# Row maxima of two key chunks taken as a couple: relu of their difference on ScalarE, one fused add-and-max on VectorE

## The chip, the cores and the metric

The kernel runs on one core of one Trainium2 chip. The metric is the device time of one execution in microseconds (us). A core has five engines that each run their own instruction queue in order and wait for each other through semaphores: TensorE (PE, with PEld for its weight loads), VectorE (DVE), ScalarE (ACT), GpSimd (POOL) and SyncE (SP), which here only issues DMAs. Matmuls write to PSUM, eight banks of 128 partitions x 512 float32 values; VectorE and ScalarE read them from there.

## The reference

```python
def _A_ref(x, wqkv, wo):                      # S = 2048, D = 512, H = 32 heads of Dh = 16
    qkv = (x @ wqkv).reshape(B, S, 3, H, Dh).transpose(2, 0, 3, 1, 4)
    q, k, v = qkv[0], qkv[1], qkv[2]
    scores = einsum("bhqd,bhkd->bhqk", q, k) * Dh ** -0.5
    p = softmax(scores, axis=-1)
    o = einsum("bhqk,bhkd->bhqd", p, v)
    return o.transpose(0, 2, 1, 3).reshape(B, S, D) @ wo

def _B_ref(x, w1, b1, w2, b2):                # F = 1792
    h = layernorm(x)
    u = gelu(einsum("bsd,sf->bdf", h, w1) + b1)
    return (einsum("bdf,fs->bds", u, w2) + b2).transpose(0, 2, 1)

xn = layernorm(x)
return x + _A_ref(xn, ...) * silu(_B_ref(xn, ...))
```

Attention over 32 heads, a token-mixing MLP, and a gated sum. Inputs and outputs are float32.

## The kernel before

**Precision.** A float32 operand is kept as two float32r parts, an upper one and the remainder (`sub`, L75). A product of two such operands takes three matmuls, or one with a contraction three times as long: `load_qk` (L97) lays the 16 rows of a head's q and k in 48 rows as (upper, upper, lower) against (upper, lower, upper).

**Preparation.** The first part (to L355) normalises x in four chunks of 512 tokens, turns it, and makes q, k and v. For each chunk there are four q parts and four k parts, of 128 rows each; a part's twelve matmuls go to a PSUM bank, ScalarE copies the upper half into a tile `sg`, VectorE subtracts the lower one, and a DMA writes both to HBM (`q_d`, `k_d`). Between the parts VectorE works off a list `todo`: the normalisation of the next chunk (`first`) and a second one for the mixer (`second`), whose result ScalarE and GpSimd split into the tiles `hb`. `hb` takes all sixteen slots of the pool `hu` at the start.

**The steps.** The rest works on pairs of heads, one on the array's rows 0 to 63 and one on 64 to 127, so that a matmul of either head runs beside one of the other. The loop over `s` (L944 on) makes one step out of two counts. Softmax is done over transposed scores (keys on the partitions), so its row maxima have to be known first, and they run `LEAD` = 20 counts ahead of the scores. One step has four maxima and four scores for each of the two heads, and work for both:

- the maxima (`max_of`, L378): queries of one block of 128 against the chunks 0 to 3 of 512 keys, each a matmul (L387) into a bank `mx` and a `tensor_reduce` (L391) on VectorE into a column of `mxp`
- the scores (`score`): a matmul (L757) into a bank `sc`, and an Exp on ScalarE (L762). Two extra rows of q hold the negated maximum
- two value bursts, each for both heads (`values`, eight matmuls at L773), from scores of the step before
- and some products of the mixer (L911), each split into two matmuls of 64 rows, one on each head's rows

The banks `mx` and `sc` are three each, handed round in order: a matmul into a bank waits for the reader of the product three before it in the same pool. The accumulators `av` and `dn` have one bank each.

`wanted` says how many mixer products a step gets: mostly six, otherwise five, four or two. All of them go in one run (a burst of mixer products) on one head's rows first, the lead's, and then in another on the other's. The order in a step is written out by hand in `ORDERS`; D is a mixer product, m a maxima product, s a score product. The first string is that of the lead, the second that of the other head, and the pairs are issued one by one; the number is the pair ahead of which the value burst of the middle stands:

```python
2: ("smsmDDsmsm", "msmsmsmsDD", 3),
4: ("sDDDDmsmsmsm", "msmsmsmDDDDs", 6),
6: ("DDDDDDsmsmsmsm", "msmsmsmsDDDDDD", 7),
```

So a step falls into two halves, each ahead of one value burst, and `lead` is turned round in each step that has mixer products. Of a step with six products, the first half holds the other head's four maxima and three of its scores, and one score of the lead; the second half the lead's four maxima.

After eight steps `max_rows` (L393) takes the maximum over the four columns of `mxp`, and `turn` moves it into the rows of q (a transpose at L402, a copy, two GpSimd instructions and four DMAs on GpSimd's queue).

**Before and after the steps.** Ten steps come first with maxima and mixer products alone (`first_maxima`), and ten follow the last maxima, with scores and the output product (`rest`, matmuls at L886). The last pair of heads is finished by `own` (L606): its `move_in` brings the first half of that pair's result into an operand tile with four DMAs on GpSimd's queue, and sets `own_done`, for which the generator `rest` waits ahead of the products that read the tile.

`later` and `after(n, f)` put off `f` to the n-th call of `run_later`; there are two calls in each step.

Of the kernel before, what the change touches and what calls it, by code (L numbers as in the profile page):

```python
# [21 lines left out]
def tile_attention_token_mixer(ctx, tc, x, wqkv, wo, w1, b1, w2, b2, out):  # L22
    nc = tc.nc
# [31 lines left out]
    q_d = [dram.tile([P, 2, S], F32R, name=f"q_d{g}") for g in range(ND)]  # L55
    k_d = [dram.tile([P, 2, S], F32R, name=f"k_d{g}") for g in range(ND)]
    v_d = dram.tile([NB, P, NP * 48], F32, name="v_d")
    u_d = [dram.tile([P, 2, D], F32R, name=f"u_d{i}") for i in range(NF)]
# [13 lines left out]
    xv = x.rearrange("(b p) d -> p b d", p=P)  # L72
    hb = [hu.tile([P, 2, D], F32R, name="hu") for _ in range(NB)]

# [12 lines left out]

    qs, ks, vps = {}, {}, {}

# [7 lines left out]
    def load_qk(p):  # L97
        if p > 1:
            qs[p], ks[p] = qs[p - 2], ks[p - 2]
        q, k = qs[p], ks[p]  # L100
        for a in range(2):
            g, r0 = divmod((2 * p + a) * DH, P)
            rows = slice(r0, r0 + DH)
            o = 64 * a

            for n in range(2):
                move(k[o + DH * n : o + DH * (n + 1), :], k_d[g][rows, n, :])
                move(q[o + DH * n : o + DH * (n + 1), :], q_d[g][rows, 0, :])
            move(k[o + 2 * DH : o + 3 * DH, :], k_d[g][rows, 0, :])
            move(q[o + 2 * DH : o + 3 * DH, :], q_d[g][rows, 1, :])  # L110
# [40 lines left out]
    with (  # L151
# [88 lines left out]
        def second(c):  # L240
            def then(b, o):
                h = hb[4 * c + b]
# [28 lines left out]
        for c in range(NC):  # L271
# [23 lines left out]
            for n, (part, g) in enumerate(order):  # L295
                m = slice(g * P, (g + 1) * P)
                ps = bank()
                for w, z in ((wh, 0), (wh, 1), (wl, 0)):
                    for kd in range(ND):
# [60 lines left out]
    sm = pool("sm", 2, reuse_waits="tile")  # L360
    el = pool("el", 2, reuse_waits="tile")

    later = []
# [13 lines left out]

    def max_of(u, half, a, pl=ps_mx, nm="mx"):  # L378

        p, r = divmod(u // 2, NB)  # L380
        c = u % 2 * 2 + half
        if u // 16 not in mxp:
            mxp[u // 16] = sm.tile([P, 2, 8, NC], F32, name="mxp")
        q, k = qs[p], ks[p]
        o = 64 * a
        ps = pl.tile([P, 512], F32, name=nm)
        nc.tensor.matmul(  # L387
            ps, q[o : o + 48, r * P : (r + 1) * P], k[o : o + 48, c * 512 : (c + 1) * 512],
            start=True, stop=True,
        )  # L390
        nc.vector.tensor_reduce(mxp[u // 16][:, a, r % 8, c : c + 1], ps, axis=AX.X, op=OP.max)  # L391

# [210 lines left out]
    asides = []  # L603
    own_done = [False]

    def own(span, ev):  # L606
# [34 lines left out]
        def move_in():  # L641
# [139 lines left out]
    def rest():  # L781
# [32 lines left out]
        for n, b in enumerate(blocks):  # L814
            if n == NB // 2:
                yield from until(lambda: own_done[0] and (ND - 1, 0) in divided)
            ps = ps_dn.tile([P, 512], F32, name="dn")[:, :D]
# [126 lines left out]
    for s in range(0, total + 1, 2):  # L944
# [8 lines left out]
        if s < NU and t >= 0:  # L953
# [24 lines left out]
            for f in then:  # L978
                f()
        elif s < NU:  # L980

# [107 lines left out]
```

## Time and profile before

| | |
|---|---|
| median of 3 runs | 1706.81 us (1706.4 to 1709.35) |
| the profiled execution: its time | 1709.11 us |
| the profiled execution: its span | 1707.3 us |
| mean granted TensorE clock | 0.995 |

The busy time of the engines in stretches of the span, from the view of windows (a busy TensorE is not TensorE at its peak):

| stretch, us | what runs | PE | DVE | ACT | POOL |
|---|---|---|---|---|---|
| 60 to 120 | preparation | 60.00 | 38.21 | 22.13 | 16.08 |
| 600 to 800 | steps | 198.70 | 175.62 | 150.08 | 71.13 |
| 1200 to 1400 | steps | 199.64 | 177.03 | 152.34 | 56.72 |
| 1650 to 1707 | end | 40.70 | 25.10 | 27.04 | 6.95 |

How rows are read. In a row of the timeline stand the start and the duration in us, the engine, the line of the kernel, the operation with output and inputs, and xN for N of them merged; in brackets the engine's idle time before and what ended it. In the page's groups stand the busy time, the mean of one in ns, and the engine's idle time before them with its main releaser. VectorE's and ScalarE's instructions overlap their neighbours of the same engine a little, so that the mean of one is longer than the distance between two. The chain of waits is the work that ended last, followed back from the end.

### The profile page before, as it was taken

What the parts mean: (1) busy time and instruction counts of PE and PEld (TensorE: products, weight loads), DVE (VectorE), ACT (ScalarE), POOL (GpSimd) and SP (SyncE); (2) the same over time, 40 slices, a digit from 0 to 9 for tenths busy, and PEclk for the clock granted to TensorE, in tenths of its full rate; (3) what the DMA queues carried; (4) which work ended last, traced back from release to release, by engine and by line L of the source; (5) the groups of instructions that cost most, each with busy time, mean ns of one, the idle gap of its engine ahead of it and who ended that gap; (6) DMA issues with size and microseconds to landing.
All of it is one profiled execution on the core that took longest, in us unless ns stands there. A gap on an engine that the chain in (4) does not pass through costs nothing.

```text
span 1707.3 us, 30652 instructions
## 1 busy us (share of the span) xinstructions
PE 1672.8 (98%) x11716; PEld 846.9 (50%) x11716; DVE 1409.7 (83%) x2378; ACT 1187.9 (70%) x2291; POOL 567.1 (33%) x673
## 2 busy tenths in 40 slices
PE   7999999999999999999999999999999999999987
PEld 6887644444444444444444444444444444444443
DVE  6565888888888888888888888888888888888834
ACT  3333277777777777777777777777777777787845
POOL 4223842233342334333422322222222222463401
PEclk9999999999999999999999999999999999999999
DMA  6467611415150514353332415141515132272435
GB/s 222 179 235 184 133 44 42 75 44 85 45 85 20 92 46 68 135 127 94 75 60 64 79 35 82 36 80 31 81 33 82 37 48 52 78 158 85 147 98 186
DMA packets 150879, 152.94 MB, mean 90 GB/s; under 512 B 51452, under 2 KB 109820, under 8 KB 147660
## 3 DMA queue, kind: packets, MB, share of 16 engines
q1 hardware_dynamic: 146188, 149.97, 36.8%
q0 software_dynamic: 4544, 1.01, 0.4%
q8 instruction: 92, 1.51, 0.4%
q14 instruction: 55, 0.45, 0.1%
HBM read 100.29 MB, written 49.53 MB: 88 GB/s over the span
## 4 chain that ended last, share of the span: by engine, by line
PE 92%; DVE 5%; ACT 1%; DMA 0%; issue 0%; POOL 0%; SPq 0%; DVEq 0%; POOLq 0%
PE av L773 28%; PE dn L911 26%; PE mx L387 13%; PE sc L757 12%; DVE mxp L391 4%; PE dn L886 3%; PE mx L300 2%; PE sc L300 2%; ACT prob L762 1%; PE av L886 1%; PE av L300 1%; PE dn L300 1%; PE mx L757 1%; PE mx L402 0%; PE sc L83 0%
## 5 line engine op out<-in xcount | busy, mean ns | idle before, releaser
L391 DVE TENSOR_REDUCE mxp<-mx 128x1 f32<-128x512 f32 x2008 | 1250.5, 683 | 183.9 <-PE mx L387 97.4
L762 ACT ACTIVATE prob<-sc 128x512 f32<-128x512 f32 x2008 | 1041.8, 604 | 331.1 <-PE sc L757 252.6
L387 PE MATMUL mx<-big 48*128 48x512 f32 x2008 | 826.8, 428 | 2.1
L757 PE MATMUL sc<-big 50*128 50x512 f32 x2008 | 771.8, 428 | 3.4 <-DMA big<-m 2.0
L911 PE MATMUL dn<-hu,wh 64*128 64x512 f32 x1570 | 573.8, 406 | 0.0
L773 PE MATMUL av<-prob,vp 128*32 128x512 f32 x4096 | 546.3, 605 | 0.0
L387 PEld LDWEIGHTS mx<-big 48*128 48x128 f32 x2008 | 364.2, 186 | 221.8 <-DVE mxp L391 206.6
L757 PEld LDWEIGHTS sc<-big 50*128 50x128 f32 x2008 | 355.1, 185 | 191.7 <-ACT prob L762 173.3
L911 PEld LDWEIGHTS dn<-hu,wh 64*128 64x128 f32 x1570 | 289.3, 185 | 171.5 <-issue 145.5
L911 PE MATMUL dn<-hu,wl 64*128 64x512 f32 x786 | 316.3, 402 | 0.0
L145 POOL CAST wh<-raw 128x512 fp32r<-128x512 f32 x108 | 62.8, 582 | 327.3 <-PE dn L911 309.6
L76 POOL TENSOR_TENSOR wl<-raw,wh 128x512 fp32r<-128x512 f32 x124 | 150.3, 1215 | 38.6 <-ACT wh L147 29.9
L773 PEld LDWEIGHTS av<-prob,vp 128*32 128x32 f32 x4096 | 81.0, 108 | 150.6 <-issue 138.6
L911 PEld LDWEIGHTS dn<-hu,wl 64*128 64x128 f32 x786 | 145.9, 186 | 8.3 <-issue 0.8
L406 POOL CAST m<-f 16x128 fp32r<-16x128 f32 x32 | 9.0, 280 | 266.1 <-DVE f L405 266.1
L464 POOL TENSOR_TENSOR sq<-u 128x512 f32<-128x512 f32 x14 | 14.6, 1040 | 170.9 <-ACT u L463 170.9
L80 POOL DMA_DIRECT2D big<-m x128 | 67.7, 535 | 0.0
L762 ACT ACTIVATE prob<-mx 128x512 f32<-128x512 f32 x40 | 25.1, 627 | 29.2 <-PE sc L757 22.0
L500 POOL TENSOR_SCALAR t<-t 128x512 f32<-128x512 f32 x16 | 23.8, 1488 | 62.4 <-ACT t L497 62.4
L911 PE MATMUL dn<-wh,hu 64*128 64x512 f32 x120 | 41.6, 399 | 0.0
L76 POOL TENSOR_TENSOR hu<-hx,hu 128x512 fp32r<-128x512 f32 x16 | 20.4, 1291 | 54.6 <-ACT hu L243 54.6
L300 PE MATMUL mx<-xt,big 128*128 128x512 f32 x144 | 35.4, 395 | 0.0
(202 smaller groups left out, 1094.2 us busy)
## 6 DMA issues: line engine op xcount, KB each, us to landing
raw<-in_B_w_dram SPq DMA_DIRECT2D x104, 256.0 KB
big<-k_d SPq DMA_DIRECT2D x96, 128.0 KB
big<-q_d SPq DMA_DIRECT2D x96, 128.0 KB
q_d<-sg SPq DMA_DIRECT2D x16, 512.0 KB
k_d<-sg SPq DMA_DIRECT2D x16, 512.0 KB
num_d<-ev SPq DMA_DIRECT2D x30, 256.0 KB
u_d<-uo SPq DMA_DIRECT2D x14, 512.0 KB
hu<-u_d SPq DMA_DIRECT2D x14, 512.0 KB
```

The source lines that it names most:

```text
L76: eng.tensor_tensor(out=o, in0=a, in1=b.bitcast(F32), op=OP.subtract)
L80: queue.dma_start(dst.bitcast(F32), src.bitcast(F32))
L145: nc.gpsimd.tensor_copy(whs[n][:, :m, :], raws[n][:, :m, :])
L300: nc.tensor.matmul(ps, w[part][:, kd, m], xt[kd][:, z, :], start=w is wh and z == 0 and kd == 0, stop=w is wl and kd == ND - 1,)
L387: nc.tensor.matmul(ps, q[o : o + 48, r * P : (r + 1) * P], k[o : o + 48, c * 512 : (c + 1) * 512], start=True, stop=True,)
L391: nc.vector.tensor_reduce(mxp[u // 16][:, a, r % 8, c : c + 1], ps, axis=AX.X, op=OP.max)
L500: nc.gpsimd.tensor_scalar(t, t, 1.0, None, op0=OP.add)
L757: nc.tensor.matmul(ps, ks[p][o : o + 50, kb * P : (kb + 1) * P], qs[p][o : o + 50, at : at + 512], start=True, stop=True,)
L762: nc.scalar.activation(e, ps, AF.Exp, scale=scale)
L773: nc.tensor.matmul(av[32 * j : 32 * j + 32, :], vps[p][:, kb, 16 * a : 16 * a + 32], prob.pop((t, a, c)), start=kb == 0, stop=kb == NB - 1,)
L886: nc.tensor.matmul(ps, w(slice(0, P)), m(slice(0, P)), start=first, stop=last)
L911: made.append(lambda r=r, start=first and a == lead, stop=last and a != lead: nc.tensor.matmul(ps, w(r), m(r), start=start, stop=stop,))
```

## The change

Keys of chunk 0 and 1 of a head are k0 and k1. For each query, max(q·k0, q·k1) = q·k1 + max(0, q·(k0 - k1)), element by element over the 512 keys. For the head that does not lead, in each step that has scores, the kernel now uses this:

- in the preparation it makes d = k0 - k1 in the second chunk's k parts (two VectorE operations, a ScalarE copy and a GpSimd subtraction for its two parts) and keeps it in HBM (`kd_d`). For this the first chunk's k parts are held in `first_k`, four slots of the pool `hu`; `hb` takes its slots one by one
- `load_qk` loads the difference of each pair of heads into a tile `kd`, with six more DMAs; that of the first pair is loaded ahead of the steps
- the maxima product of chunk 0 becomes the product with `kd`, into a bank of `sc` in place of `mx`; ScalarE's Relu takes it to a tile `above` in SBUF
- the reduction of chunk 1 becomes a `tensor_tensor_reduce`, which adds `above` to the product and takes the maximum; column 0 of `mxp` is not written by this and keeps the lowest value, which GpSimd sets when a new `mxp` is begun
- `lead` is turned round at the end of the step, since the maxima look at it when they are issued. The strings of the order stay with the same heads as before
- `own_done` is set two calls of `run_later` later

```diff
-    hb = [hu.tile([P, 2, D], F32R, name="hu") for _ in range(NB)]
+    first_k = [hu.tile([P, 2, 512], F32R, name="hu") for _ in range(ND)]
+    hb = {}
...
         q, k = qs[p], ks[p]
+        if p:
+            kds[p] = kdp.tile([P, 512], F32R, name="kd")
...
+                if p:
+                    move(kds[p][o + DH * n : o + DH * (n + 1), :], kd_d[g][rows, n, :])
+            if p:
+                move(kds[p][o + 2 * DH : o + 3 * DH, :], kd_d[g][rows, 0, :])
...
-                sg = pst.tile([P, 2, 512], F32R, name="sg")
+                sg = first_k[g] if part and c == 0 else pst.tile([P, 2, 512], F32R, name="sg")
...
+                if part and c == 1:
+
+                    k0 = first_k[g]
+                    d = pst.tile([P, 512], F32, name="hx", bufs=2)
+                    nc.vector.tensor_tensor(out=d, in0=k0[:, 0, :].bitcast(F32), in1=ps, op=OP.subtract)
+                    nc.vector.tensor_tensor(out=d, in0=d, in1=k0[:, 1, :].bitcast(F32), op=OP.add)
+                    nc.scalar.copy(k0[:, 0, :], d)
+                    sub(nc.gpsimd, k0[:, 1, :], d, k0[:, 0, :])
+                    move(kd_d[g], k0)
...
+    kdp = pool("kdp", 2, reuse_waits="tile")
+    rl = pool("rl", 2, reuse_waits="tile")
+    kds[0] = kdp.tile([P, 512], F32R, name="kd")
+    for a in range(2):
+        for n, part in enumerate((0, 1, 0)):
+            row = 64 * a + DH * n
+            move(kds[0][row : row + DH, :], kd_d[0][DH * a : DH * (a + 1), part, :])
...
-    def max_of(u, half, a, pl=ps_mx, nm="mx"):
+    above = {}
+    LOWEST = -3.0e38
+
+    def max_of(u, half, a, pl=ps_mx, nm="mx", couple=False):
...
             mxp[u // 16] = sm.tile([P, 2, 8, NC], F32, name="mxp")
+            nc.gpsimd.memset(mxp[u // 16], LOWEST)
         q, k = qs[p], ks[p]
         o = 64 * a
+        if couple and c == 0:
+
+            ps = ps_sc.tile([P, 512], F32, name="sc")
+            nc.tensor.matmul(
+                ps, q[o : o + 48, r * P : (r + 1) * P], kds[p][o : o + 48, :], start=True, stop=True,
+            )
+            above[a] = rl.tile([P, 512], F32, name="above")
+            nc.scalar.activation(above[a], ps, AF.Relu)
+            return
...
-        nc.vector.tensor_reduce(mxp[u // 16][:, a, r % 8, c : c + 1], ps, axis=AX.X, op=OP.max)
+        most = mxp[u // 16][:, a, r % 8, c : c + 1]
+        if couple and c == 1:
+            up = above.pop(a)
+            nc.vector.tensor_tensor_reduce(
+                out=up, in0=ps, in1=up, scale=1.0, scalar=LOWEST, op0=OP.add, op1=OP.max, accum_out=most,
+            )
+        else:
+            nc.vector.tensor_reduce(most, ps, axis=AX.X, op=OP.max)
...
-            own_done[0] = True
+            after(2, lambda: own_done.append(True))
...
-                mx.append(lambda i=i: max_of(s + i // 2, i % 2, a))
+                mx.append(lambda i=i: max_of(s + i // 2, i % 2, a, couple=s >= LEAD and a != lead))
...
-            if one:
-                lead = 1 - lead
+            turned_round = bool(one)
...
             for f in then:
                 f()
+            if turned_round:
+                lead = 1 - lead
```

More of the change, by code (lines that the diff above doesn't have):

```diff
@@ L56, in tile_attention_token_mixer @@
     k_d = [dram.tile([P, 2, S], F32R, name=f"k_d{g}") for g in range(ND)]
+    kd_d = [dram.tile([P, 2, 512], F32R, name=f"kd_d{g}") for g in range(ND)]
     v_d = dram.tile([NB, P, NP * 48], F32, name="v_d")
@@ L85, in three @@
         nc.tensor.matmul(ps, wl, mh, start=False, stop=last)
-    qs, ks, vps = {}, {}, {}
+    qs, ks, kds, vps = {}, {}, {}, {}
     def place_qk(p):
@@ L241, in then @@
             def then(b, o):
-                h = hb[4 * c + b]
+                h = hb[4 * c + b] = hu.tile([P, 2, D], F32R, name="hu")
                 nc.scalar.copy(h[:, 0, :], o)
@@ L603, in tile_attention_token_mixer @@
     asides = []
-    own_done = [False]
+    own_done = []
     def own(span, ev):
@@ L815, in rest @@
             if n == NB // 2:
-                yield from until(lambda: own_done[0] and (ND - 1, 0) in divided)
+                yield from until(lambda: own_done and (ND - 1, 0) in divided)
             ps = ps_dn.tile([P, 512], F32, name="dn")[:, :D]
```

## The prediction

> **What bounds the kernel now.** I read the page first: busy shares, the chain that ended last, the costliest groups.
>
> ```profile
> span 1707.3 us, 30652 instructions
> ...
> PE 1672.8 (98%) x11716; PEld 846.9 (50%) x11716; DVE 1409.7 (83%) x2378; ACT 1187.9 (70%) x2291; POOL 567.1 (33%) x673
> ...
> PE 92%; DVE 5%; ACT 1%; DMA 0%; issue 0%; POOL 0%; SPq 0%; DVEq 0%; POOLq 0%
> ...
> L391 DVE TENSOR_REDUCE mxp<-mx 128x1 f32<-128x512 f32 x2008 | 1250.5, 683 | 183.9 <-PE mx L387 97.4
> L762 ACT ACTIVATE prob<-sc 128x512 f32<-128x512 f32 x2008 | 1041.8, 604 | 331.1 <-PE sc L757 252.6
> ```
>
> TensorE holds 92% of the chain, VectorE 5%. So the question is whether TensorE runs at its own pace or is paced by the PSUM banks that the other two hand back. Shares can't tell; the timeline of one step can. This is a step of the commonest kind (six mixer products on each head's rows), with its waits for banks:
>
> ```profile
> 612.73 0.18 PEld L911 LDWEIGHTS dn<-hu,wh 64*128 64x128 f32 x1 [0.84 <-issue]
> ...
> 613.30 2.48 DVE L391 TENSOR_REDUCE mxp<-mx 128x1 f32<-128x512 f32 x4 [0.43 <-PE mx L387]
> ...
> 613.53 2.07 ACT L762 ACTIVATE prob<-sc 128x512 f32<-128x512 f32 x4 [1.04 <-PE sc L757]
> ...
> 614.18 0.18 PEld L757 LDWEIGHTS sc<-big 50*128 50x128 f32 x1 [0.20 <-ACT prob L762]
> ...
> 614.61 0.16 PEld L773 LDWEIGHTS av<-prob,vp 128*32 128x32 f32 x8 [0.24 <-issue]
> ...
> 615.60 0.18 PEld L387 LDWEIGHTS mx<-big 48*128 48x128 f32 x1 [0.84 <-DVE mxp L391]
> ...
> 616.17 2.06 ACT L762 ACTIVATE prob<-sc 128x512 f32<-128x512 f32 x4 [0.58 <-PE sc L757]
> ...
> 617.48 0.16 PEld L773 LDWEIGHTS av<-prob,vp 128*32 128x32 f32 x8 [0.36 <-issue]
> ```
>
> Each half of a step is a value burst (0.99 us from its first weight load to the next one, 614.61 to 615.60) and then 1.88 us of pairs, two row halves of the array at a time. I count from the first weight load after the burst. At 0.57 the first maxima product is ready and VectorE begins; at 0.80 ScalarE begins its first Exp. Both then wait idle for TensorE at the next half (0.43 and 0.58 to 1.04 us), so neither has a backlog. The one late bank is a score bank: the fourth score product of the half needs the bank of the first, and its weights load at 1.45, 0.65 after that Exp began. The burst follows 0.43 later. VectorE is late nowhere here: four reductions in 2.48 us fit a half of 2.88.
>
> In steps with four and with two products per head, the waits are larger:
>
> ```profile
> 229.61 0.18 PEld L757 LDWEIGHTS sc<-big 50*128 50x128 f32 x1 [0.84 <-ACT prob L762]
> ...
> 230.15 1.57 ACT L762 ACTIVATE prob<-sc 128x512 f32<-128x512 f32 x3 [0.79 <-PE sc L757]
> ...
> 230.93 0.18 PEld L387 LDWEIGHTS mx<-big 48*128 48x128 f32 x1 [0.31 <-DVE mxp L391]
> ```
> ```profile
> 640.53 0.16 PEld L773 LDWEIGHTS av<-prob,vp 128*32 128x32 f32 x8 [0.38 <-issue]
> 641.53 0.18 PEld L757 LDWEIGHTS sc<-big 50*128 50x128 f32 x1 [0.84 <-ACT prob L762]
> ...
> 642.43 0.16 PEld L773 LDWEIGHTS av<-prob,vp 128*32 128x32 f32 x8 [0.37 <-issue]
> 643.43 0.18 PEld L387 LDWEIGHTS mx<-big 48*128 48x128 f32 x1 [0.84 <-DVE mxp L391]
> ...
> 644.00 2.56 ACT L762 ACTIVATE prob<-sc 128x512 f32<-128x512 f32 x5 [0.36 <-PE mx L387]
> ...
> 645.14 0.18 PEld L757 LDWEIGHTS sc<-big 50*128 50x128 f32 x1 [0.24 <-ACT prob L762]
> ```
>
> The last row is the key. That half sends five products through the three score banks; ScalarE begins at 0.57, and the fifth product's weights load at 645.14 - 643.43 = 1.71. That is 0.57, one step of ScalarE (2.56 for five with 0.61 for the last: 0.485 each), and 0.65 until the bank is taken again.
>
> **The change part by part.** *The couple.* Chunk 0 of the other head (the one not leading) leaves the maxima banks and VectorE for a score bank and ScalarE. The other head's four maxima stand in the first half of a step with six or four products, and its first two in the first half of one with two. So every first half gets one more product through the score banks: five in place of four, or four in place of three. The second halves keep their four or five, and the order of the products on TensorE is otherwise the same.
>
> Six products, or five, which run in the same order (178 of the 246 steps with maxima and scores, 2008 = 246 x 8 + 40 Exps). The difference product is first in the half, so Relu begins at 0.57 and Exp at 0.57 + 0.485 = 1.055. The fourth user of the banks needs Relu's, at 0.57 + 0.65 = 1.22, about when it is issued now. The fifth needs that of the first Exp: 1.055 + 0.65 = 1.705, where the last score product now loads at 1.45. The burst behind it slides by 0.255. Nothing covers it: the products of that half are all issued ahead. 178 x 0.255 = 45.4 us.
>
> Four products (39 steps). The lead's score product comes first, so Exp begins at 0.57, Relu at 1.055, and the last score product needs Relu's bank: 1.705, against 1.32 today (230.93 - 229.61, there a maxima bank, which the change relieves). 39 x 0.385 = 15.0 us.
>
> Two products (28 steps). The first half has three pairs and no wait now: its burst comes at 0.90 (642.43 - 641.53). With four users the last needs the first Exp's bank: 0.57 + 0.65 = 1.22, and 0.43 more to the burst, 1.65. 28 x 0.75 = 21.0 us.
>
> Together +81.4 us. I counted the kinds by the weight loads between bursts along the timeline; the first and last burst ahead of a first half of each kind, in the order six, four, two:
>
> ```profile
> 222.86 0.16 PEld L773 LDWEIGHTS av<-prob,vp 128*32 128x32 f32 x8 [0.25 <-issue]
> ...
> 1597.50 0.16 PEld L773 LDWEIGHTS av<-prob,vp 128*32 128x32 f32 x8 [0.24 <-issue]
> ```
> ```profile
> 217.37 0.16 PEld L773 LDWEIGHTS av<-prob,vp 128*32 128x32 f32 x8 [0.40 <-issue]
> ...
> 1592.02 0.16 PEld L773 LDWEIGHTS av<-prob,vp 128*32 128x32 f32 x8 [0.37 <-issue]
> ```
> ```profile
> 280.06 0.16 PEld L773 LDWEIGHTS av<-prob,vp 128*32 128x32 f32 x8 [0.37 <-issue]
> ...
> 1608.44 0.16 PEld L773 LDWEIGHTS av<-prob,vp 128*32 128x32 f32 x8 [0.24 <-issue]
> ```
>
> Relu has no row. Its step is bounded by 0.47 and 0.57, from Identity, copy and Exp in direct succession (0.56 and 0.47 here) and Tanh before Exp; I take 0.485, since nothing else in these rows depends on the function. At 0.57 the sum grows by 0.085 x 217 = 18 us.
>
> ```profile
> 440.86 0.73 ACT L463 ACTIVATE u<-dn,b1t 128x512 f32<-128x512 f32 x1
> ...
> 441.42 0.64 ACT L512 COPY ev<-av 128x512 f32<-128x512 f32 x1
> ...
> 441.89 0.67 ACT L762 ACTIVATE prob<-sc 128x512 f32<-128x512 f32 x1
> ```
>
> The Trainium skill, "ScalarE: Activation LUTs", section "What ACT_TABLE_LOAD costs", gives an ACTIVATE with immediates 186 ns + 0.833 ns per element, less about 93 ns where one follows another: an estimate of 0.52 us here. The rows say 0.485 and are used; by the page the sum would be 0.035 x 217 = 7.6 us larger.
>
> *VectorE's side.* One TENSOR_REDUCE fewer per step, and a reduction that adds and takes the maximum in one. That operation has no row: not below one subtraction from PSUM (0.687), not above that and a TENSOR_REDUCE (0.683), 1.37 together; I take 0.75, nearest to the single pass. It waits for Relu, so it begins at about 1.23, and with two reductions behind it VectorE is free at 1.23 + 0.75 + 1.2 = 3.2, before the next half's first maxima at 2.12 + 0.99 + 0.57 = 3.7. At 1.37 it is free at 3.8, and the fourth maxima product of the second half finds its bank at 4.5, needed at about 4.6. So no cost up to the bound, and no gain either, because TensorE did not wait for VectorE in these steps. In the others the waits that it relieves (1.32 above) lie below the new one.
>
> ```profile
> L76 DVE TENSOR_TENSOR sg<-sc,sg x12: 670/687/693, 30.4 to 140.5; 128x512 fp32r<-128x512 f32 x12
> ```
>
> *Preparation.* In the second of four chunks each of four K parts gains two VectorE passes, a ScalarE copy (0.6), a GpSimd subtraction (1.3) and a DMA. GpSimd is idle there. VectorE's 8 x 0.6 = 4.8 us delay what follows on it, down to the last lower half of the turned tiles:
>
> ```profile
> 81.48 0.69 DVE L76 TENSOR_TENSOR xt<-sc,xt 128x512 fp32r<-128x512 f32 x1 [1.55 <-ACT xt L267]
> ```
> ```profile
> 83.57 2.72 PE mx L300 x12
> ```
>
> That tile is ready at 82.17 and first read by the eighth of these twelve products, at 83.57 + 7 x 0.227 = 85.2: 3.0 us of cover. +2 us, between 0 and 6. The loads of the differences (6 more issues on SP's queue per pair of heads, at about 0.45 each) come six steps ahead of their use: 0, at most 3 at the start, where they stand ahead of weight loads. GpSimd's memset (one per eight steps) is ahead of the first maxima by program order: 0. Turning `lead` round at the end of the step moves no instruction by itself.
>
> *The end.* `own_done` is now set two bursts later. Today TensorE stands before a product whose operand GpSimd's DMA has yet to bring, and is slow behind it:
>
> ```profile
> 1657.52 0.29 PEld L886 LDWEIGHTS dn<-wh,hu 128*128 128x128 f32 x1 [6.02 <-issue]
> ...
> 1659.82 0.20 PEld L773 LDWEIGHTS av<-prob,vp 128*32 128x32 f32 x8 [0.44 <-issue]
> ...
> 1664.38 0.16 PEld L773 LDWEIGHTS av<-prob,vp 128*32 128x32 f32 x8 [0.37 <-issue]
> ...
> 1669.48 0.16 PEld L773 LDWEIGHTS av<-prob,vp 128*32 128x32 f32 x8 [0.36 <-issue]
> ```
>
> The burst ahead of the stall began 6.02 + 0.16 before 1657.52, at 1651.3: 13.0 us to 1664.38, where the next two halves with the same work take 5.1. Two halves of scores now go first, so the products come at about 1656.5 and wait 1 us. That is -7 us, between -3 and -9.
>
> Sum: +81.4 + 2 - 7 = +76.4. Against the profiled execution: 1707.3 + 76.4 = 1783.7 of span, 1709.1 + 76.4 = 1785.5 of its time; the median of the runs, 1706.8, lies 2.3 below that execution, so 1783.
>
> **The rivals.**
> *VectorE's relief decides (faster).* If Relu's and Exp's banks came back within 0.88 us of Relu's start (they need 0.485 + 0.65 = 1.135), the fifth product would not be late, and the waits on VectorE would be the ones to go: 39 first halves shrink from 1.75 (1.32 + 0.43) to one pair less than 1.88, 1.65: -3.9 - 7 + 2 = -9, so 1698. For it: TensorE's weight loads stood 0.31 us behind VectorE in the row at 230.93. Against it: the row at 645.14. The Trainium skill, "VectorE: DVE Perf Modes", section "Rules for kernel authors", calls `tensor_reduce` the slowest operation of that engine and advises restructuring; by that rule this rival is right, and the trace bears it out only where maxima banks are late.
> *The edit is hidden.* If the burst could pass the late product, only end and preparation would show: -5, 1702. TensorE issues in order in every row, so this is unlikely.
> *Relu and Exp don't overlap.* A step of 0.65 in place of 0.485 adds 0.165 x 217 = 36: 1819. The succession at 441.42 speaks against it.
> *The fused reduction is long.* From 1.4 us on it delays the second half's banks one for one; at 2 us that is 0.5 x 246 = 123 more, 1906. Only its missing row speaks for it.
>
> **How the numbers follow.** Forecast 0.80, relief 0.06, hidden 0.03, no overlap 0.06, long reduction 0.05. The likeliest gives 1783; its unknown terms span 1766 (end -9, preparation 0, a bank back 0.05 us earlier) to 1812 (step 0.57, preparation +6, start +3). To hold 8 in 10 with the near rival I take 1753 to 1820. What a measurement of this kernel can tell from no change is about 0.2%, 3.4 us. Faster 0.08 (relief, and hidden but for 0.01), same 0.01, slower 0.91.
>
> **What would show it.** Right: first halves of 3.1 us with five ScalarE operations, a score weight load that waits on ScalarE at 1.7 after the burst, second halves still 2.88; steps with two products at 6.0 in place of 5.3; VectorE's share down, its idle time before the fused operation put down to ScalarE; no 6 us gap near the end. Wrong: first halves of 2.88, or waits of maxima weight loads on VectorE grown, which would mean the fused operation; or a stall at the start of the 246 steps.

## The result, and the profile after

| | before | after |
|---|---|---|
| median, same chip, 4 runs each | 1707.86 us (1706.4 to 1709.35) | 1813.59 us (1810.93 to 1816.43) |
| ratio, 95% interval | | 1.0619 (1.0599 to 1.0639) |
| span of the profiled execution | 1707.3 us | 1814.3 us |

Slower by 105.7 us, where 76 had been forecast: inside the range (1753 to 1820), 30 above the number. From the page of the kernel after (its span, its busy shares, the chain's shares by engine, and three groups with busy time, mean in ns and idle time before them with its releaser):

```profile
span 1814.3 us, 31521 instructions
...
PE 1747.9 (96%) x11716; PEld 872.5 (48%) x11716; DVE 1277.4 (70%) x2386; ACT 1306.7 (72%) x2541; POOL 576.1 (32%) x709
...
PE 84%; ACT 7%; DVE 4%; DMA 2%; issue 2%; POOL 1%; SPq 0%; DVEq 0%; POOLq 0%; ACTq 0%
...
L431 DVE CUSTOM_DVE_ANT_0 above<-mx,above 128x512 f32<-128x512 f32 x246 | 170.2, 692 | 263.9 <-PE sc L801 142.1
...
L435 DVE TENSOR_REDUCE mxp<-mx 128x1 f32<-128x512 f32 x1516 | 954.7, 684 | 164.8 <-PE sc L801 104.9
...
L421 ACT ACTIVATE above<-sc 128x512 f32<-128x512 f32 x246 | 147.3, 599 | 133.8 <-PE sc L417 113.7
```

The work has gone where the edit sends it: VectorE is busy for 132 us less, ScalarE for 119 us more. The fused operation takes 692 ns, hardly longer than the reduction that it replaces (683). ScalarE's part of the chain has risen from 1% to 7%.

Three rows of the timeline after cut the span into stretches: the weight load of the first maxima product, the first Exp, and the weight load of the last maxima product.

```profile
162.48 0.18 PEld L424 LDWEIGHTS mx<-big 48*128 48x128 f32 x1 [0.35 <-issue]
...
225.98 0.59 ACT L806 ACTIVATE prob<-sc 128x512 f32<-128x512 f32 x1
...
1725.50 0.18 PEld L424 LDWEIGHTS mx<-big 48*128 48x128 f32 x1 [0.41 <-DVE mxp L435]
```

The same rows of every trace give a table that the rest of this text uses (us; profiled executions; the one of the kernel after is the longest of its four, 1816.43):

| | preparation | first ten steps | steps with both | end |
|---|---|---|---|---|
| before | 153.3 | 54.7 | 1405.2 | 94.1 |
| after | 162.5 | 63.5 | 1499.5 | 88.8 |
| difference | +9.1 | +8.8 | +94.3 | -5.3 |

So most of it lies in the steps, as forecast; but preparation and the first ten steps cost 18 where 2 had been put down.

A first half with six products, in the timeline after. (The long idle times ahead of Relu and of the fused operation come from the slow stretch just before this half, shown further down; from 320.40 on the granted clock is 1.00.)

```profile
320.60 0.18 PEld L417 LDWEIGHTS sc<-kd,big 48*128 48x128 f32 x1
...
321.16 0.60 ACT L421 ACTIVATE above<-sc 128x512 f32<-128x512 f32 x1 [1.42 <-PE sc L417]
...
321.66 2.06 ACT L806 ACTIVATE prob<-sc 128x512 f32<-128x512 f32 x4
321.80 0.69 DVE L431 CUSTOM_DVE_ANT_0 above<-mx,above 128x512 f32<-128x512 f32 x1 [2.02 <-PE sc L801]
...
322.30 0.18 PEld L801 LDWEIGHTS sc<-big 50*128 50x128 f32 x1 [0.31 <-ACT prob L806]
...
322.41 1.28 DVE L435 TENSOR_REDUCE mxp<-mx 128x1 f32<-128x512 f32 x2
322.74 0.16 PEld L817 LDWEIGHTS av<-prob,vp 128*32 128x32 f32 x8 [0.25 <-issue]
```

Counted from 320.60: Relu at 0.56, the first Exp 0.50 behind it, and the last score product's weights at 1.70 (1.705 in the forecast, 1.45 before). Such halves take 3.13 to 3.14 us (2.87 before), second halves 2.88 as before. VectorE is through with its three passes at 323.69, before the next maxima.

The first half of a two-product step after:

```profile
633.01 0.16 PEld L817 LDWEIGHTS av<-prob,vp 128*32 128x32 f32 x8 [0.37 <-issue]
...
634.54 0.60 ACT L806 ACTIVATE prob<-sc 128x512 f32<-128x512 f32 x1 [0.79 <-PE sc L801]
...
635.04 0.59 ACT L421 ACTIVATE above<-sc 128x512 f32<-128x512 f32 x1
635.20 0.18 PEld L801 LDWEIGHTS sc<-big 50*128 50x128 f32 x1 [0.89 <-ACT prob L806]
...
635.62 0.16 PEld L817 LDWEIGHTS av<-prob,vp 128*32 128x32 f32 x8 [0.24 <-issue]
...
639.00 0.16 PEld L817 LDWEIGHTS av<-prob,vp 128*32 128x32 f32 x8 [0.31 <-issue]
```

2.61 and 3.38 make a step of 5.99, the 6.0 of the forecast: the last score product waits 0.89 us for the bank of the first Exp.

What had not been forecast at all is this place in the timeline after, the first step of a new block of eight, with the turn of the old one (L446; the first and the last row are value bursts):

```profile
306.67 1.06 PE L817 MATMUL av<-prob,vp 128*32 128x512 f32 x8
...
308.07 1.04 POOL L508 TENSOR_TENSOR sq<-u 128x512 f32<-128x512 f32 x1 [24.51 <-ACT u L507]
...
311.11 0.61 POOL L153 CAST wh<-raw 128x512 fp32r<-128x512 f32 x1
311.80 1.26 POOL L78 TENSOR_TENSOR wl<-raw,wh 128x512 fp32r<-128x512 f32 x1
313.00 0.15 POOL L411 MEMSET mxp<- 128x64 f32 x1
...
313.19 0.69 DVE L431 CUSTOM_DVE_ANT_0 above<-mx,above 128x512 f32<-128x512 f32 x1 [5.02 <-POOL mxp L411]
...
313.94 0.38 PE L446 MATMUL mx<-ident,neg 128*16 128x128 f32 x1 [4.12 <-DVE mxp L431]
...
314.25 1.94 PE L817 MATMUL av<-prob,vp 128*32 128x512 f32 x8
```

The memset itself takes 0.15 us. But GpSimd works in order, and five operations of the mixer, about 4.9 us, stand ahead of it. VectorE waits 5.02 us for it, TensorE 4.12 us for VectorE. The value burst behind the idle time takes 1.94 us in place of 1.06, and the half that it begins 4.73 in place of 2.74. TensorE is slow for a while behind the stall: the view of windows gives it a granted clock of 0.50 from 313.94 to 318.98 (1.00 from 306.67 to 309.67), and 1.00 again from 320.40 on. The Trainium skill, "TensorE: Matmul & The Clock Gate", section "Part 1: The HAM clock gate", says that at least one idle window of about 3.4 us halves the clock and that at least one busy window of as much brings it back. The halving behind a stall of 4.12 us agrees; the way back took some 6.4 us here.

### The profile page after: what moved, and what is told of

It reads as the page before. It is cut to its first block, busy times and chain, and to the rows that moved or that the text cites. A ratio compares the mean times of both kernels' runs of the same rounds, so it can differ in the third digit from the quotient of the medians.

```text
span 1814.3 us, 31521 instructions
## 1 busy us (share of the span) xinstructions
PE 1747.9 (96%) x11716; PEld 872.5 (48%) x11716; DVE 1277.4 (70%) x2386; ACT 1306.7 (72%) x2541; POOL 576.1 (32%) x709
## 4 chain that ended last, share of the span: by engine, by line
PE 84%; ACT 7%; DVE 4%; DMA 2%; issue 2%; POOL 1%; SPq 0%; DVEq 0%; POOLq 0%; ACTq 0%
PE av L817 27%; PE dn L955 21%; PE sc L801 15%; PE mx L424 13%; ACT prob L806 4%; PE dn L930 3%; PE mx L308 1%; PE sc L308 1%; ACT ev L540 1%; DVE mxp L435 1%; PE mx L801 1%; DMA xr<-in_A_x_dram 1%; DVE st L210 0%; PE mx L446 0%; DMA big<-q_d 0%
## 5 line engine op out<-in xcount | busy, mean ns | idle before, releaser
L435 DVE TENSOR_REDUCE mxp<-mx 128x1 f32<-128x512 f32 x1516 | 954.7, 684 | 164.8 <-PE sc L801 104.9
L801 PE MATMUL sc<-big 50*128 50x512 f32 x2008 | 830.7, 439 | 17.4 <-ACT prob L806 15.4
L424 PE MATMUL mx<-big 48*128 48x512 f32 x1762 | 721.8, 427 | 3.2 <-DVE mxp L435 1.2
L424 PEld LDWEIGHTS mx<-big 48*128 48x128 f32 x1762 | 315.7, 187 | 220.5 <-DVE mxp L435 179.6
L431 DVE CUSTOM_DVE_ANT_0 above<-mx,above 128x512 f32<-128x512 f32 x246 | 170.2, 692 | 263.9 <-PE sc L801 142.1
L421 ACT ACTIVATE above<-sc 128x512 f32<-128x512 f32 x246 | 147.3, 599 | 133.8 <-PE sc L417 113.7
L417 PE MATMUL sc<-kd,big 48*128 48x512 f32 x246 | 121.6, 494 | 0.2 <-ACT prob L806 0.2
L417 PEld LDWEIGHTS sc<-kd,big 48*128 48x128 f32 x246 | 45.0, 183 | 0.5 <-ACT prob L806 0.5
```

Of the source, the lines that this page charges most:

```text
L417: nc.tensor.matmul(ps, q[o : o + 48, r * P : (r + 1) * P], kds[p][o : o + 48, :], start=True, stop=True,)
L421: nc.scalar.activation(above[a], ps, AF.Relu)
L424: nc.tensor.matmul(ps, q[o : o + 48, r * P : (r + 1) * P], k[o : o + 48, c * 512 : (c + 1) * 512], start=True, stop=True,)
L431: nc.vector.tensor_tensor_reduce(out=up, in0=ps, in1=up, scale=1.0, scalar=LOWEST, op0=OP.add, op1=OP.max, accum_out=most,)
L435: nc.vector.tensor_reduce(most, ps, axis=AX.X, op=OP.max)
L801: nc.tensor.matmul(ps, ks[p][o : o + 50, kb * P : (kb + 1) * P], qs[p][o : o + 50, at : at + 512], start=True, stop=True,)
```

## The experiments

All ratios are to the kernel before on the same chip (medians of 1706.35 to 1708.56 us).

**The end alone.** The kernel before, with the two calls of delay for `own_done` and nothing else.

```diff
-            own_done[0] = True
+            after(2, lambda: own_done.append(True))
```

> The kernel before with `own_done` set two calls of `run_later` later, and nothing else. Theory: the stall ahead of the products of the last pair of heads (6.02 us idle and slow matmuls behind it) is replaced by two halves of scores, 7 us less (4 to 9), about 1700.5. Rival: the products only move to where nothing is left to run beside them, and the time stays within 2 us of before.

Measured: 1703.41 us, 0.9972 (0.9961 to 0.9983), 4.3 us saved, and the fastest of all kernels here. More than the rival's 2, less than the 7 of the forecast. In its trace the 6 us stall is gone, but a smaller one has come where it was:

```profile
1657.01 0.19 PEld L886 LDWEIGHTS dn<-wh,hu 128*128 128x128 f32 x1 [2.73 <-issue]
...
1658.32 1.94 PE L773 MATMUL av<-prob,vp 128*32 128x512 f32 x8
...
1660.18 0.29 PEld L886 LDWEIGHTS dn<-wh,hu 128*128 128x128 f32 x1 [1.66 <-DVE xt L734]
```

The value burst behind it takes 1.94 us, as slow as the one behind the memset's stall. The 1.66 ahead of the next weight load is that burst and no stall of its own, and this load takes 0.29 in place of 0.19.

**Everything but the couple.** The kernel after, where no maxima product is coupled; the differences are still made and loaded.

```diff
-                mx.append(lambda i=i: max_of(s + i // 2, i % 2, a, couple=s >= LEAD and a != lead))
+                mx.append(lambda i=i: max_of(s + i // 2, i % 2, a, couple=False))
```

> The changed kernel with no couple taken: the preparation of the differences, their loads, the memset of `mxp` on GpSimd and the later `own_done` stay, and all eight maxima of a step go through the maxima banks and VectorE as before. Theory (the couple costs 81 us by ScalarE's extra place ahead of the scores' banks, the rest costs what the two traces differ by outside the halves): halves back at 2.88 and 2.74, preparation +9, first ten steps +8, waits on the memset some 14, end -5: about 1733. Rival (most of the 106 us are the preparation, loads and waits on GpSimd): 1770 or more.

Measured: 1736.06 us, 1.0158 (1.0143 to 1.0174). So the couple by itself costs 1813.6 - 1736.1 = 77.5, and what comes with it 28. Halves with six, four and two products take what they took before (2.88, 2.74 to 2.95, and 1.90). Stalls on the memset remain (two halves of 8.3, one of 5.16, one of 4.21). In the stretches: preparation +9.2, first ten steps +8.1, steps +18.3, end -6.9.

**The memset on VectorE.** The kernel after with one word changed.

```diff
-            nc.gpsimd.memset(mxp[u // 16], LOWEST)
+            nc.vector.memset(mxp[u // 16], LOWEST)
```

> The changed kernel with the memset of `mxp` issued on VectorE in place of GpSimd. Theory (the memset stands behind the GELU and the weight splits in GpSimd's queue, and VectorE's first maximum of a group waits for it): the halves of 7.6 and 4.7 us at two places of the steps shrink to 3.3 and 2.75, VectorE no longer waits for GpSimd, some 14 us less in the steps and 3 to 5 in the first ten, so 1794 to 1798. Rival (those halves are long for the weights' own splits on GpSimd): within 4 us of the changed kernel, 1813.

Measured: 1795.3 us, 1.0511 (1.0497 to 1.0526): 18.3 us less. The half with the stall shown above (306.67 to 314.25, 7.58 us) takes 3.61, and the first ten steps 56.7 in place of 63.5. Of the 18.8 between the two profiled executions 6.8 lie in the first ten steps, 9.7 in the steps and 2.3 in the preparation, where seven executions with the same preparation differ by 4; so the memset costs 16 to 18 us. There the memset is a row of 0.11 us on VectorE. The steps are left at 1489.9, +84.6, where the forecast had +81.4.

**The difference in a maxima bank.** The kernel after; the difference product goes through the banks `mx`, so that no half sends more products through `sc` than before. Relu still stands first in ScalarE's queue.

```diff
-            ps = ps_sc.tile([P, 512], F32, name="sc")
+            ps = pl.tile([P, 512], F32, name=nm)
```

> The changed kernel with the product of the difference in a maxima bank, as chunk 0 was before; ScalarE's Relu reads it there. The score banks have four users in a half again. Theory (what counts is that ScalarE reaches the first Exp one place later): the last score product still waits until 1.7 us after the burst with six and four products (halves of 3.13 and 3.1), and only steps with two products, whose maxima and scores are three each in the first half, go back from 2.6 to 1.9: 28 x 0.7 = 20 us less, 1794. Rival (what counts is that five products share three score banks): all first halves go back to 2.88, 2.75 and 1.9, some 80 us less, 1735.

Measured: 1796.04 us, 1.0518 (1.0504 to 1.0532). First halves of two-product steps are back at 1.90. Those with six products are not; one of them, in this kernel's timeline:

```profile
318.62 0.16 PEld L817 LDWEIGHTS av<-prob,vp 128*32 128x32 f32 x8 [0.39 <-issue]
...
320.18 0.60 ACT L421 ACTIVATE above<-mx 128x512 f32<-128x512 f32 x1 [0.84 <-PE mx L417]
...
320.68 1.57 ACT L806 ACTIVATE prob<-sc 128x512 f32<-128x512 f32 x3
...
321.32 0.18 PEld L801 LDWEIGHTS sc<-big 50*128 50x128 f32 x1 [0.48 <-ACT prob L806]
...
321.75 0.16 PEld L817 LDWEIGHTS av<-prob,vp 128*32 128x32 f32 x8 [0.24 <-issue]
```

3.13 again. With four products through three score banks, the fourth waits for the first Exp's bank, and that Exp begins 0.50 later because Relu is ahead of it. So in these steps what counts is not how many products share the banks, but at which place ScalarE reaches the first Exp.

**ScalarE's part alone.** The kernel before; chunk 0 of the other head goes through a score bank, a copy on ScalarE takes it to SBUF, and VectorE reduces it from there. No difference, no memset, `own_done` as before; VectorE keeps all eight reductions. As in the kernel after, the other head is told by `lead`, which is turned round at the end of the step.

```diff
+        aside = couple and c == 0
+        ps = ps_sc.tile([P, 512], F32, name="sc") if aside else pl.tile([P, 512], F32, name=nm)
...
+        if aside:
+            above = rl.tile([P, 512], F32, name="above")
+            nc.scalar.copy(above, ps)
+            ps = above
```

> The kernel before with ScalarE's part of the change alone: in each step with scores, chunk 0 of the head that does not lead goes to a score bank, ScalarE copies it to SBUF, and VectorE reduces it from there. VectorE keeps its eight reductions; no difference, no loads, no memset, `own_done` as before. Theory (the extra ScalarE operation ahead of the scores' banks is what the couple costs, and VectorE's relief is worth nothing): 178 x 0.25 + 39 x 0.36 + 28 x 0.72 = 79 us more than before, 1787. Rivals: VectorE's relief was worth something, then this is slower than that by it (VectorE waits for the copy and then has four reductions, so up to 0.2 us a half, 1835); or the couple's cost lay in the fused operation and the memset, then it stays below 1760.

Measured: 1815.51 us, 1.0637 (1.0622 to 1.0653), 28 above the theory and 20 below the first rival's 1835. First halves with six products take 3.13 and two-product ones 2.61, exactly as in the kernel after, so ScalarE's place alone makes those. The extra time is VectorE's. At a step with a turn, in this kernel's timeline:

```profile
440.28 0.59 ACT L395 COPY above<-sc 128x512 f32<-128x512 f32 x1 [0.84 <-PE sc L389]
...
440.90 0.69 DVE L397 TENSOR_REDUCE mxp<-above 128x1 f32<-128x512 f32 x1 [0.82 <-ACT above L395]
...
441.50 1.88 DVE L397 TENSOR_REDUCE mxp<-mx 128x1 f32<-128x512 f32 x3
...
442.24 0.09 PEld L408 LDWEIGHTS mx<-ident,neg 128*16 128x16 f32 x1 [0.63 <-DVE mxp L397]
```

VectorE waits for the copy ahead of its four reductions, and the turn waits for VectorE: 3.73 us for the half, 3.34 after, 3.11 before. Second halves of two-product steps take 3.59 (3.37 before). The largest part, some 12 us against the kernel before, lies in the second halves of four-product steps: 3.11 for 2.74, with three waits of 0.30 for maxima banks that VectorE holds. In the steps this kernel stands at 1513.4, the one with the memset on VectorE at 1489.9: the fused reduction does save time, some 24 us between these two kernels, but only against a delay that ScalarE's operation brings with it. So the first rival has a part in it: VectorE's relief is worth something as soon as VectorE is made late.

**The first load later; both; and more.** Three attempts at the rest. The first pair's six loads twelve counts later:

```diff
-    for a in range(2):
-        for n, part in enumerate((0, 1, 0)):
-            row = 64 * a + DH * n
-            move(kds[0][row : row + DH, :], kd_d[0][DH * a : DH * (a + 1), part, :])
...
+    after(12, load_kd0)
```

> The changed kernel with the six loads of the first pair's differences issued twelve counts later, behind the weights' first loads on SP's queue. Theory (in the first ten steps TensorE waits for weights whose loads stand behind those six): the first ten steps shrink from 62.5 us to some 58, 4 us less, 1809. Rival (those steps wait for the memset and for slots of the weights alone): no change, 1813.

Measured: 1814.11 us, 1.0627 (1.0611 to 1.0643): no change. The loads ahead of the weights cost nothing that shows here. With the memset on VectorE as well, by the one word shown above:

> The changed kernel with both mends: memset on VectorE, the first pair's loads later. Theory: the sum of the two, 18 to 22 us less, 1791 to 1795, of which 80 over the kernel before less 5 at the end and plus 9 in the preparation are left. Rival (one of the two only uncovers the other wait): as the better of the two alone.

Measured: 1797.01 us, 1.0523 (1.0508 to 1.0539), as the memset alone. With the difference in a maxima bank too, and made by GpSimd from `sg` in the preparation:

```diff
-                    nc.vector.tensor_tensor(out=d, in0=k0[:, 0, :].bitcast(F32), in1=ps, op=OP.subtract)
-                    nc.vector.tensor_tensor(out=d, in0=d, in1=k0[:, 1, :].bitcast(F32), op=OP.add)
-                    nc.scalar.copy(k0[:, 0, :], d)
+                    sub(nc.gpsimd, d, k0[:, 0, :].bitcast(F32), sg[:, 0, :])
+                    nc.gpsimd.tensor_tensor(out=d, in0=d, in1=k0[:, 1, :].bitcast(F32), op=OP.add)
+                    sub(nc.gpsimd, d, d, sg[:, 1, :])
+                    nc.gpsimd.tensor_copy(k0[:, 0, :], d)
```

> The changed kernel with the memset on VectorE and the product of the difference in a maxima bank; the preparation builds the difference with four GpSimd operations in place of VectorE's two and ScalarE's copy, and the first pair's loads are issued later. Theory: 20 us less by the steps with two products, 14 to 18 by the memset, 4 by the loads, and 0 to 9 in the preparation: 1763 to 1775. It stays above the kernel before, since the first halves with six and four products still wait for ScalarE. Rival: GpSimd's longer work in the preparation holds up the second normalisation and costs 10 us more there.

Measured: 1785.39 us, 1.0458 (1.044 to 1.0475), 10 above the theory, on the side of its rival: preparation takes 167.7, which is 5.2 worse than after where the rival had 10. In this kernel's chain of waits GpSimd's work takes most of the time up to 91.87, and the next chunk's products begin at 95.28 (90.18 after, 83.57 before):

```profile
90.60 1.27 POOL hu L78
...
95.28 5.37 PE mx L308 x12
```

**Relu in the third place.** The kernel after with the difference in a maxima bank, and the coupled head's maxima in the order chunk 2, chunk 3, difference, chunk 1.

```diff
+        apart = s >= LEAD and a != lead
...
-                mx.append(lambda i=i: max_of(s + i // 2, i % 2, a, couple=s >= LEAD and a != lead))
+                j = (2, 3, 0, 1)[i] if apart else i
+                mx.append(lambda j=j: max_of(s + j // 2, j % 2, a, couple=apart))
```

> The changed kernel with two edits: the difference product goes to a maxima bank (as in the run before with that edit alone), and the coupled head's four maxima are issued in the order chunk 2, chunk 3, difference, chunk 1, so that Relu stands behind two Exps in ScalarE's queue and the first Exp begins as early as before. The theory (what costs is the place of Relu ahead of the first Exp, not ScalarE's additional work): halves with six products back to 2.88, with two to 1.90, so that only GpSimd's memset, the preparation and the end are left, as in the kernel without the couple: 1731 to 1738. The rival (an additional ScalarE operation that is released by TensorE and releases VectorE costs its step wherever it stands): no less than 1780, near the 1796 of the run with the bank alone. A second rival (the fused reduction becomes late because it waits for a Relu that comes later): halves that wait for VectorE, 1750 to 1780.

Measured: 1764.93 us, 1.033 (1.0316 to 1.0344), 31 less than with the bank alone, though 27 above the theory. A six-product first half in this kernel's timeline:

```profile
320.81 0.16 PEld L817 LDWEIGHTS av<-prob,vp 128*32 128x32 f32 x8 [0.36 <-issue]
...
322.62 1.09 ACT L806 ACTIVATE prob<-sc 128x512 f32<-128x512 f32 x2 [1.05 <-PE dn L955]
...
323.27 0.18 PEld L801 LDWEIGHTS sc<-big 50*128 50x128 f32 x1 [0.22 <-ACT prob L806]
...
323.59 0.60 ACT L421 ACTIVATE above<-mx 128x512 f32<-128x512 f32 x1
...
323.70 0.16 PEld L817 LDWEIGHTS av<-prob,vp 128*32 128x32 f32 x8 [0.24 <-issue]
```

2.89, with the same Relu, the same fused reduction and ScalarE as busy as before it was moved. (The new order also gives VectorE its first maxima earlier; but the row that set the half waited for ScalarE, 0.48 with the bank alone and 0.22 here.) The miss has a place: in two-product steps the order moves the difference into the second half, which has five scores already; those halves take 3.85 in place of 3.37, in 25 of the 28 steps, 25 x 0.48 = 12 us. The steps stand 25 above those of the kernel without the couple (1448.7 against 1423.5). The time lies in the second rival's range, and a part of it is that rival's: second halves of four-product steps take 2.86 in place of 2.74, where a maxima product waits 0.42 for the bank that the fused reduction holds, some 5 us. The other 8 I can't assign to one kind. The trace shows, for one, single halves of 3.84 where a maxima product waits 0.79 for the bank that Relu holds.

**The difference made in place.** The kernel after; the difference is made in the tile of the first chunk's part and not in the two slots `hx`, which the second normalisation uses too. Its two parts then lie the other way round there, and go to HBM with two DMAs.

```diff
-                    d = pst.tile([P, 512], F32, name="hx", bufs=2)
-                    nc.vector.tensor_tensor(out=d, in0=k0[:, 0, :].bitcast(F32), in1=ps, op=OP.subtract)
+                    d = k0[:, 0, :].bitcast(F32)
+                    nc.vector.tensor_tensor(out=d, in0=d, in1=ps, op=OP.subtract)
...
-                    nc.scalar.copy(k0[:, 0, :], d)
-                    sub(nc.gpsimd, k0[:, 1, :], d, k0[:, 0, :])
-                    move(kd_d[g], k0)
+                    nc.scalar.copy(k0[:, 1, :], d)
+                    sub(nc.gpsimd, k0[:, 0, :], d, k0[:, 1, :])
+                    for z in range(2):
+                        move(kd_d[g][:, z, :], k0[:, 1 - z, :])
```

> The changed kernel, where the preparation makes the difference in the tile that already holds the first chunk's k part, and not in the two slots of the second normalisation; the number of operations is the same (one more DMA for each of four parts). The theory (the normalisation waits for slots that GpSimd's subtraction of the difference still reads): the first maxima at 153 to 157 in place of 162.5, so 1804 to 1810. The rival (VectorE's two passes for each part cost it by themselves): the first maxima still at 158 to 163, 1811 to 1816.

Measured: 1811.34 us, 1.06 (1.0586 to 1.0615): 2.3 less, and the first maxima at 158.9: the rival's ranges, at their lower ends. The seven kernels that share the preparation of the kernel after started their maxima between 158.3 and 162.5 in their profiled executions, so a part of 2 or 3 us for the shared slots is possible and not shown.

**All of it mended.** Relu in the third place except in two-product steps, the difference in a maxima bank and made in place, the memset on VectorE.

> The run with Relu in the third place (1764.9), and three edits more: steps with two products keep the order difference, chunk 1, 2, 3; the memset is VectorE's; the preparation makes the difference in place. The theory (the terms add): second halves of the two-product steps 3.43 in place of 3.85, 28 x 0.42 = 12; memset 18; preparation 2: 1729 to 1737, still 1.3% to 1.7% above the kernel before, for the preparation and the halves in which ScalarE has other work too. The rival (VectorE's relief shows once nothing else is in the way, as the waits of maxima loads on VectorE in four-product steps go): down to 1715 or less. A second rival (the memset hides behind the same waits as the order's): 1745 or more.

Measured: 1724.89 us, 1.0107 (1.0091 to 1.0124), 4 below the theory's range and 10 above the rival's. Preparation 157.3, first ten steps 56.2, steps 1420.8, end 88.7. The mends take away 88.7 of the 105.7 us, nearly all of it by the places at which operations stand in their queues and banks (the difference made in place had given 2.3). Of the 17 left, the stretches give preparation +4.0, first ten steps +1.5, steps +15.6 and end -5.4 (15.7 in all, between two profiled executions); without the later `own_done`, which saved 4.3 by itself, some 21 would be left by this estimate.

## Why the prediction was right

The main mechanism was read off one row of the kernel before (the fifth product's weights at 1.71), and it held to a hundredth of a microsecond. The total did less well: 1813.6 lies inside the range but above 1812, the end to which the forecast's own terms reached, so that the range held by the margin around them. The terms beside what was measured; the first three rows are each first half against the same half of the kernel before, in the run with the memset on VectorE:

| term | predicted, us | measured, us |
|---|---|---|
| six- and five-product first halves | 178 x 0.255 = 45.4 | 47.0 in 177 |
| two-product first halves | 28 x 0.75 = 21.0 | 18.8 (25 x 0.71, and 3 with a turn at 0.34) |
| four-product first halves | 39 x 0.385 = 15.0 | 16.2 (14.0 in the 34 with four products and no turn) |
| GpSimd's memset | 0 | 16 to 18 |
| preparation | +2 (0 to 6) | +9.1 (5 to 9 in seven traces) |
| end | -7 (-3 to -9) | -4.3 |

**The steps** were right in mechanism and in sum: +81.4 forecast; 82.0 measured in the first halves, and +84.6 for the whole stretch, once the memset is out of the way. That the sum is so close is in part luck: the errors of the three terms, +1.6, -2.2 and +1.2, cancel. In one point the reason was too wide. "Five products through the three score banks" is the cause only in two-product steps, where a maxima bank for the difference gave the 0.71 back. With six products the fourth score is the late one even when only four use the banks, because the first Exp begins a place later; the run with Relu third shows the other side of it. The step also said that the coupled head's four maxima all stand in the first half of a four-product step; it is three there and one behind the burst, which doesn't change the wait.

Four-product halves come in two kinds, and only one was priced. Sixteen of the 34 take 3.09 or 3.10: nine of them took about 2.74 before, +0.35, near the 0.385 worked out, and seven took 2.79 to 2.91. Fourteen take 3.43 or 3.44 and took 2.93 to 2.96 before, +0.49, and their rows after show why:

```profile
911.75 0.16 PEld L817 LDWEIGHTS av<-prob,vp 128*32 128x32 f32 x8 [0.31 <-issue]
...
912.75 0.18 PEld L801 LDWEIGHTS sc<-big 50*128 50x128 f32 x1 [0.84 <-ACT prob L806]
...
913.11 0.63 ACT L541 ACTIVATE t<-ev 128x512 f32<-128x512 f32 x1
...
913.64 0.58 ACT L806 ACTIVATE prob<-sc 128x512 f32<-128x512 f32 x1
...
914.12 0.59 ACT L421 ACTIVATE above<-sc 128x512 f32<-128x512 f32 x1
914.27 0.18 PEld L801 LDWEIGHTS sc<-big 50*128 50x128 f32 x1 [0.57 <-ACT prob L806]
...
914.76 0.18 PEld L801 LDWEIGHTS sc<-big 50*128 50x128 f32 x1 [0.19 <-ACT above L421]
```

The mixer's Tanh stands ahead of the Exp there, which begins at 0.89 after the first weight load and not at the 0.57 of the forecast. It did so before too, and the last score product's weights then came at 1.52; with Relu behind the Exp they come at 2.01, one step of ScalarE later.

**VectorE's side** held: 692 ns (0.75 taken), no gain and no loss in the halves that set the time. The Trainium skill, "VectorE: DVE Perf Modes", section "Rules for kernel authors", advises to restructure `tensor_reduce`; here the restructured form is no faster (692 against 684 ns), and one pass fewer shortened no kind of half in the kernel after. (In the run of ScalarE's part alone, where VectorE is late, the pass is worth something.) The rival that rested on that relief (1698) falls, and so do those of an edit that is hidden (1702), of no overlap between Relu and Exp (0.50 apart, not 0.65) and of a long reduction.

**The memset is the step that failed.** "Ahead of the first maxima by program order: 0" looked at the order of the program and not at the queue. What stood in front of it on GpSimd, and who waited behind it, had to be named, as had been done for VectorE and ScalarE. It costs 16 to 18 us, more than half of the 30 by which the forecast was low; most of the rest is the preparation.

**The preparation** was mis-sized. The forecast let 3.0 of VectorE's 4.8 us hide and took GpSimd to be idle there; but in the kernel before GpSimd works on the second normalisation in this chunk, at 73.53 and at 77.08, for 2.5 us each. In the chain of waits after, the difference stands in one row of work with the normalisation that shares VectorE and GpSimd with it:

```profile
80.53 0.70 DVE hx L322
...
81.95 1.30 POOL hu L78
...
83.27 1.51 DVE hx L227
...
90.18 5.25 PE mx L308 x12
```

The twelve products start at 90.18 in place of 83.57, 6.6 us later, and behind that idle time they take 5.25 in place of 2.72, at a granted clock of 0.50 from 88.20 to 94.90. That is the 9.1 of this execution. The slow start behind a stall had been counted at the end of the kernel, and not here. Which of the two engines in that row comes first is not settled: taking the passes from VectorE and giving them to GpSimd made it worse, and making it in place gave 2.3, no more than executions of the same preparation differ by.

**The end** went the right way and gave 4.3 of 7, since a smaller stall came up where the large one was, with a slow burst behind it.

## What to carry to other kernels

Where an engine hands banks back in order, a new operation costs by its place in that engine's queue: ask which bank the next product is waiting for, and put the new operation behind the one that frees it. The same operations cost 31 us less behind two Exps than ahead of them. An instruction of no length on an in-order queue costs what stands ahead of it, so for each one added, name the longest work that can be there and who waits; and relieve only an engine that something waits for.

## What was not expected of the hardware

- The fused add and maximum is two instructions in the trace, the pass (692 ns) and a read of its accumulator (0.08 us), and reads a bank and an SBUF tile at the rate at which TENSOR_REDUCE reads a bank alone (684 ns).
- Relu and Exp follow each other on ScalarE at 0.48 to 0.50 us, and Exp follows Exp at 0.48 to 0.49, so the change of function costs at most 0.02 us here.
- A stall of 4.12 us doubled the burst behind it (1.94 for 1.06) and lengthened the half that this burst begins by 2.0 us and the one after it by 0.6 (3.76 for 3.13), together more than half of the stall's own length.
